# A gated linear recurrence and a maxout feed-forward layer: the same 821 steps in another order, on other engines, in other PSUM banks

## The chip, the cores and the metric

The kernel runs on one core of one Trainium2 chip. Its engines run side by side, each through its own queue in order: TensorE (PE in the profile, with weight loads as PEld), VectorE (DVE), ScalarE (ACT), GpSimd (POOL) and SyncE (SP), which here only issues DMAs. The metric is the device time of one execution in microseconds, as a median over runs. Before the change it is 150.05 us (3 runs: 149.97, 150.05, 151.45).

## The reference

```python
def _attn_ref(q, k, v, alpha):              # each 4 x 8 x 768 x 48
    for t in range(S):
        state = alpha[:, :, t, :, None] * state + np.einsum('bhd,bhe->bhde', k[:, :, t], v[:, :, t])
        y[:, :, t] = np.einsum('bhd,bhde->bhe', q[:, :, t], state)
    return y

def _moe_ref(x, w1, w2, w3, w_out):         # x is 3072 x 384, w1 to w3 384 x 768, w_out 768 x 384
    h = np.maximum(np.maximum(x @ w1, x @ w2), x @ w3)
    return h @ w_out
```

The output y of the first, with its heads side by side, is the x of the second. All arrays are float32.

## The kernel before

**Tiling.** The sequence of 768 is cut into three chunks of 256 rows; with four batches that makes 12 *batches* n (chunk n // 4, batch n % 4), each of two *units* u (four heads each). Inside a batch there are two sub-chunks of 128 rows. The recurrence is computed by blocks of 64 rows: the logarithms of alpha are summed along the rows by a matmul, q and k are scaled by exponentials of the sums, a matmul gives the masked products inside a block, and a carried state per batch gives the part from earlier blocks. The feed-forward layer then takes the 256 rows of a batch. It computes max(x w1, x w2, x w3) as x w1 plus max(0, x(w2 - w1), x(w3 - w1)), and the part x w1 w_out by one product matrix *past*.

**Steps.** The function builds a plan: each call of `plan.step` notes one step (its kind, the engines that may do it, what it reads and writes, its PSUM banks), in 821 numbers. Most steps are one instruction; a PE step is a group of matmuls. For one batch, in order of data flow, with the engine and the line of the instruction:

| kind | what | engine, line |
|---|---|---|
| load | alpha, q, k, v of a batch (halves for batch 0) | SP L278 |
| aa, la | product of neighbouring alphas, logarithms | POOL or DVE L355, ACT L360, L365 |
| hp, e, G | totals, their exponentials, state factors | PE L375, ACT L382, POOL or DVE L387, L392 |
| Lp, L0, exp, exq | sums along rows, and exp(-sum), exp(sum) | PE L430, DVE L434, ACT L445, L448 |
| q, k, v | scaled q, k, v in 16 bits | POOL or DVE L441; v POOL L265 or ACT L263 |
| tp, qkT | transposes of q and k, their copy to SBUF | PE L476, DVE L490 |
| A, LA | products inside a block, masked copy | PE L502, DVE L510 |
| pp, add, Z, Zu | state sums and state update | PE L534, DVE L404, L416, L554, POOL L404, L561 |
| yi, ya | output from the state, and from the block | PE L583, L605 |
| xb, xp, xT | scaled copy, transposing matmul, copy to x | ACT or DVE, PE L626, ACT or DVE L259 |
| gp, h0, h1 | x(w2 - w1) or x(w3 - w1), its maximum | PE L649, ACT L658 or DVE L660, DVE L665 |
| op, ob, out | past and w_out, copy, store | PE L682, L685, ACT or DVE L259, SP L701 |

Once in the kernel there are four weight loads (steps 39, 74, 86, 131; issued by POOL, L292 and L295), six differences of weights (189 to 194, DVE L312), three transposes of w1 (*wt* 195, 197, 199, PE L325, with copies 196, 198, 200) and the product matrix (*mp*, PE L338).

Of the PE steps, tp, A, pp and ya run matmuls with 64 or 48 rows in two halves of the array; hp, Lp, yi, xp, gp, op, wt and mp use all 128 rows.

**The order.** `ORDER` is a string with one token for each step, in the order in which the program is written. A token is the step's number, a letter for its engine (P, V for DVE, A, G for POOL, S) and, for a PE step that opens PSUM banks, a digit for each bank key. `Plan.emit` goes through the tokens and calls each step:

```python
            i, eng, rows = int(token[:at]), ENGINES[token[at]], token[at + 1:]
            ...
            place.update(zip(s["banks"], map(int, rows), strict=True))
            s["run"](eng)
```

So the table alone sets the order inside every engine's queue, the engine of each step that has a choice, and the bank. tp and A take two banks, the one named and the next. The framework adds the waits: an instruction waits for what it reads, and a step that opens a bank waits until what lay in it has been read. A store (out) waits for its output copy on SP, and what stands behind it on SP waits with it; an output copy waits until the store before it has read its buffer (four buffers).

Steps that the prediction names: 1, 2, 4 to 7 are the loads of q, k and v of batch 0, 53 to 56 those of batch 1. 57 is aa and 58, 59 are la of batch 1. 19 and 20 are exp and exq of unit 0, 30 and 31 of unit 1, 65 and 66 of unit 2, 77 and 78 of unit 3; 61 is e of batch 1. 21, 22 are q and k of unit 0; 32, 33, 34 are q, k, v of unit 1. 24, 35, 70 and 82 are tp of units 0 to 3, 27, 38, 73, 85 their LA; 46 and 93 are ya of batches 0 and 1. 124 is tp of units 4 and 5. 226 and 233 are v of batch 4, 241 its pp. 257, 259, 261, 263, 265, 267 are the gp of batch 0, 325 to 335 (odd) those of batch 1. 747 and 763 are gp of batches 8 and 9, 746 and 750 are h1 of batch 8. 791 and 794 are op 20 and 21, 792 and 795 their copies, 793 and 796 their stores; 797 to 807 (odd) are the gp of batch 11, 809 to 818 the last op, 819 and 820 the last copy and store. 543 and 544 are a copy and its store, 614 is the load of v of batch 10 and 637 its reader.

Of the kernel before, what the change touches and what calls it, by code (L numbers as in the profile page):

```python
# [36 lines left out]
209S 162P0 157A 282P2 205P3 163V 283A 164A 158A 201P5 167V 343S 206A 160V 165A 203P3 398A 159V 166G
276S 202V 169P0 228V 204A 136V 161A 220P4 168G 269P5 221V 210S 173V 154G 222A 229A 170V 230A 176P32
171P0 270A 277S 178V 231G 174P6 223A 177V 272P5 175V 224G 278S 172V 337P3 225G 273A 179V 232G 344S
180V 288P7 295P1 181P0 338A 289V 234P4 347G 296V 290A 182P2 238V 411S 297A 340P6 219G 298A 183V 186A  # L40
# [6 lines left out]
431P0 533P5 536A 483G 677S 432V 550A 375P3 534V 427A 463P1 549G 433A 376V 408P5 434A 313G 362A 339S
310V 369G 312V 464V 409A 428G 680S 485A 314V 484A 315V 480S 354G 435G 316P0 317P3 318P 372P4 319A
373V 377P71 476P6 551A 322A 271S 379V 436G 614S 323P4 378V 320P5 552P0 324V 438P2 321A 421G 420G
380V 553A 437A 381G 384P4 442V 486P0 597P7 548S 487A 477A 382V 489G 385P0 439V 422G 386P 491G 383V  # L50
443P5 390A 440P2 478S 488G 387A 537P1 615G 481S 441V 405P0 490G 617A 444V 430G 547S 529P2 423G 598A
538V 599P5 406A 498A 407S 492P3 388P7 679S 618P0 493V 601P1 389A 530V 619A 494A 391P7 555V 621G
# [705 lines left out]
```

## Time and profile before

| what | value |
|---|---|
| median of 3 runs | 150.05 us (149.97 to 151.45) |
| the profiled execution: its time, its span | 151.32 us, 149.6 us |
| VectorE, ScalarE, GpSimd busy | 115.9, 87.4, 73.4 us |
| mean TensorE clock granted, by the profile | 0.997 |
| DMA | 26.34 MB, 176 GB/s over the span |
| last PE matmul ends, span ends | 146.6 us, 149.6 us |

The span runs from the first to the last instruction; 1.7 us lie around it. Times in the profile are from the span's start. "L649 PE MATMUL psum<-xT,d ... x432 | 55.0, 278" is a group of instructions: line, engine, operation, what it writes and reads, count, then busy time in us and mean ns of one. Matmuls are pipelined, so the mean of one is longer than the time that it adds: in the chain of waits, six L649 matmuls behind each other add 0.66 us. In a timeline row the bracket at the end holds the idle time of the engine before the instruction, and what ended it.

### The profile page before, as it was taken

To read this page: it belongs to the slowest core of one execution; us is meant where nothing else is said; L and a number is where in the kernel's file an instruction comes from. 1 tells how busy PE (TensorE), PEld (TensorE's weight loads), DVE (VectorE), ACT (ScalarE), POOL (GpSimd) and SP (SyncE) were. 2 spreads that over 40 slices of the span, in tenths; PEclk is the share of its full clock that TensorE was granted. 3 is DMA by queue.
4 is the path that set the end of the run, shared out by engine and by line. 5 is a ranking of instruction groups with operands and counts; after the bars stand their busy time and mean duration, and the time that the engine had idled before them with its cause. 6 is when DMAs were issued, how large, how long until landed. Compare 5 with 4: busy or idle time off the path is not lost.

```text
span 149.6 us, 5638 instructions
## 1 busy us (share of the span) xinstructions
PE 133.0 (89%) x2389; PEld 103.0 (69%) x2389; DVE 115.9 (77%) x215; ACT 87.4 (58%) x194; POOL 73.4 (49%) x118
## 2 busy tenths in 40 slices
PE   0235798999999999999999999999799999999991
PEld 0014677877766768887888778877579777776861
DVE  6356988499978999999998788979889985656260
ACT  3756236894987498968868787655464123412311
POOL 8159901275235997899982649585456010000000
PEclk9999999999999999999999999999999999999998
DMA  5999999999999999999999992104111010004403
GB/s 121 253 260 264 241 213 224 265 242 214 278 254 260 242 266 256 255 269 266 277 298 273 288 284 57 57 2 161 58 53 57 0 57 0 0 4 158 158 30 127
DMA packets 54728, 26.34 MB, mean 176 GB/s; under 512 B 50736, under 2 KB 54320, under 8 KB 54704
## 3 DMA queue, kind: packets, MB, share of 16 engines
q1 hardware_dynamic: 53584, 23.60, 62.0%
q0 software_dynamic: 832, 2.36, 8.2%
q8 instruction: 18, 0.29, 0.8%
q10 hardware_dynamic: 288, 0.04, 0.2%
q14 instruction: 6, 0.05, 0.1%
HBM read 23.63 MB, written 4.72 MB: 189 GB/s over the span
## 4 chain that ended last, share of the span: by engine, by line
PE 79%; DVE 9%; DMA 5%; SPq 2%; issue 1%; POOL 1%; ACT 1%; DVEq 0%; ACTq 0%; POOLq 0%
PE psum L649 32%; PE psum L685 14%; PE psum L682 7%; PE psum L502 5%; PE psum L476 5%; PE psum L605 4%; DVE LA L510 4%; DMA kn<-in_k_dram 3%; PE psum L626 3%; PE psum L583 2%; SPq L278 2%; PE psum L338 2%; PE psum L534 2%; DVE qkT L490 2%; DMA out_dram<-ob 1%
## 5 line engine op out<-in xcount | busy, mean ns | idle before, releaser
L649 PE MATMUL psum<-xT,d 128*128 128x256 f16 x432 | 55.0, 278 | 0.0
L649 PEld LDWEIGHTS <-d 128*128 128x128 f16 x432 | 41.2, 100 | 6.8
L510 DVE TENSOR_TENSOR LA<-psum,d 128x1024 f16<-128x1024 f32 x24 | 29.0, 1219 | 2.6 <-PE psum L502 1.6
L665 DVE TENSOR_TENSOR hT<-psum,hT 128x512 f16<-128x512 f32 x36 | 23.9, 681 | 6.8 <-PE psum L649 6.5
L685 PE MATMUL psum<-wo,hT 128*128 128x384 f16 (+1 forms) x150 | 27.5, 320 | 0.0
L658 ACT ACTIVATE hT<-psum 128x512 f16<-128x512 f32 x30 | 17.7, 604 | 11.5 <-PE psum L649 10.9
L441 POOL TENSOR_TENSOR qk<-qn,ep 128x384 f16<-128x384 f32 x18 | 18.0, 1004 | 11.7 <-ACT ep L448 8.2
L441 POOL TENSOR_TENSOR qk<-kn,en 128x384 f16<-128x384 f32 x18 | 17.9, 1000 | 7.2 <-DMA kn<-in_k_dram 2.9
L259 ACT COPY ob<-psum 128x384 f32<-128x384 f32 (+1 forms) x18 | 8.3, 463 | 22.0 <-PE psum L685 18.8
L685 PEld LDWEIGHTS <-hT 128*128 128x128 f16 x150 | 14.4, 98 | 9.0 <-DVE hT L665 0.2
L490 DVE COPY qkT<-psum 128x1024 f16<-128x1024 f16 x24 | 15.7, 684 | 3.5 <-PE psum L476 3.1
L682 PE MATMUL psum<-past,xT 128*128 128x384 f16 (+1 forms) x75 | 15.9, 321 | 0.0
L263 ACT ACTIVATE xb<-psum,c 128x384 f16<-128x384 f32 x18 | 9.9, 580 | 8.4 <-PE psum L605 8.3
L259 ACT CAST xT<-psum 128x384 f16<-128x384 f32 x21 | 9.7, 488 | 8.2 <-PE psum L626 8.2
L445 ACT ACTIVATE en<-psum 128x384 f32<-128x384 f32 x24 | 11.5, 490 | 2.8 <-DVE psum L434 2.5
L434 DVE TENSOR_TENSOR psum<-psum,la 128x192 f32<-128x192 f32 x24 | 8.5, 360 | 4.4 <-PE psum L430 3.1
L502 PE MATMUL psum<-qkT 48*64 48x128 f16 x384 | 10.3, 235 | 1.3 <-DVE qkT L490 1.0
L476 PE MATMUL psum<-d,qk 64*128 64x64 f16 x384 | 8.8, 198 | 2.5 <-DVE LA L510 1.4
L561 POOL TENSOR_TENSOR Z<-U,G 48x192 f16<-48x192 f32 x11 | 5.6, 506 | 11.0 <-DVE U L554 10.6
L355 POOL TENSOR_TENSOR aa<-an 128x384 f32<-128x384 f32 x10 | 9.9, 1003 | 1.3 <-DMA an<-in_alpha_dram 1.2
L476 PEld LDWEIGHTS <-qk 64*128 64x128 f16 x384 | 7.4, 99 | 4.0 <-issue 2.8
L375 PE MATMUL psum<-c,la 128*128 128x4 f16 x48 | 3.0, 167 | 8.0 <-ACT la L365 8.0
(61 smaller groups left out, 193.7 us busy)
## 6 DMA issues: line engine op xcount, KB each, us to landing
out_dram<-ob SPq DMA_DIRECT2D x23, 192.0 KB, 2.1
an<-in_alpha_dram SPq DMA_DIRECT2D x11, 384.0 KB, 6.1
vn<-in_v_dram SPq DMA_DIRECT2D x11, 384.0 KB, 6.1
kn<-in_k_dram SPq DMA_DIRECT2D x11, 384.0 KB, 6.3
qn<-in_q_dram SPq DMA_DIRECT2D x11, 384.0 KB, 6.0
wcat<-in_moe_w_dram POOLq DMA_DIRECT2D x2, 576.0 KB, 11.7
w1s<-in_moe_w_dram POOLq DMA_DIRECT2D x1, 576.0 KB, 7.9
wo<-in_moe_w_out_dram POOLq DMA_DIRECT2D x1, 576.0 KB, 8.4
```

Source lines behind the costliest of these rows:

```text
L259: (nc.scalar.copy if eng == "ACT" else nc.vector.tensor_copy)(out=out, in_=in_)
L441: on[eng].tensor_mul(qk[:, w, :, :, :D].rearrange("p r h d -> p h r d"), ld[x][n % NL][:, hs], e)
L445: lambda eng: nc.scalar.activation(out=en, in_=live[Lk], func=AFT.Exp, scale=-1.0),
L476: nc.tensor.transpose(live["tp", v][:, i, at:at + HALF], qks[v % NQ][rows, w, r, 2 * j:2 * j + 2, :], ident[rows, rows])
L490: lambda eng: nc.vector.tensor_copy(out=qkT.rearrange("p i w j t -> p i (w j t)"), in_=live["tp", u]),
L502: nc.tensor.matmul(live[Ak][i * HALF:(i + 1) * HALF, p, at:at + P], qkT[rows, i, 1, j, r * HALF:(r + 1) * HALF], qkT[rows, i, 0, j, :], st ...
L510: lambda eng: nc.vector.tensor_mul(LA.rearrange("p a j r t -> p (a j) (r t)"), live[Ak].rearrange("p a (j t) -> p (a j) t", j=2), maskA.un ...
L649: nc.tensor.matmul(live[gk][:, jj, :], hidden(apart[g][j][:, kt], jj), xT[:, kt, :], start=(kt == 0), stop=(kt == NFT - 1))
L658: nc.scalar.activation(out=h, in_=live[gk], func=AFT.Relu)
L665: lambda eng, h=h, gk=gk: nc.vector.tensor_max(h, live[gk], h),
L682: nc.tensor.matmul(live[ok], xT[:, kt, i * P:(i + 1) * P], past[:, kt, cols], start=(kt == 0), stop=False)
L685: nc.tensor.matmul(live[ok], hT[:, kt, i * P:(i + 1) * P], wo16[:, kt, cols], start=False, stop=(kt == NJ - 1))
```

## The change

Only the string `ORDER` changes. All steps are the same. Every engine has the steps in another order. 79 steps are on another engine: among them 9 of the v from ACT to POOL and 6 the other way; 8 output copies from ACT to DVE and 3 back; 7 of the h0 from ACT to DVE and 5 back; 5 of the q each way between DVE and POOL, 2 of the k each way; aa of batch 1 from DVE to POOL. DVE gets 206 steps (200 before), ACT 184 (193), POOL 106 (103). PE keeps its 248, in another order and in other banks, and SP its 77. Among the loads, those of q, k and v of batches 0 and 1 and alpha of batches 3 and 4 change places; the stores stand elsewhere among the loads.

```diff
@@ -24,49 +24,49 @@
...
 ORDER = """
-0S 3S 1S 53S 7S 2S 5S 6S 8V 10A 4S 11V 12A 13A 56S 14P0 28P4 17P1 15A 9A 29V 16G 18V 30A 55S 19A 57V
-31A 20A 59A 21V 54S 60P5 22G 63P6 75P2 61A 58A 24P0 32G 64V 100S 25V 65A 33G 76V 26P3 77A 101S 34G
-27V 62G 23G 69A 39G 35P4 81A 102S 78A 40P37 74G 36V 66A 86G 42V 37P4 41V 80G 103S 38V 45P1 46P0 68G
-79V 67G 44V 87P45 47A 43V 50A 88V 90V 70P1 82P6 71V 51P0 83V 72P1 52A 84P6 73V 145S 104G 195P3 89V
-48P2 106A 91V 199P4 105A 85V 92P1 49A 117P5 200A 118V 93P6 189V 107P7 108A 97V 119A 257P4 109G 94A
-191V 110P1 120A 95P6 111V 98P7 190V 265P2 96A 99A 207S 197P6 112A 325P7 266A 193V 113A 121G 333P2
-198A 275S 114V 261P5 192V 258A 329P6 115V 326A 122V 147S 196A 124P0 194V 334A 263P4 128V 116G 262A
-146S 125V 131G 129P2 330A 267P7 130V 123A 149G 150A 132P06 148S 133V 126P2 134V 331P1 212A 127V 211G
-259P5 151A 137P0 213A 332V 138P2 264V 327P3 208S 142A 260V 139A 143P0 279G 155P1 144A 268V 140P4
...
-226G 235V 291A 345S 285G 349A 299G 292V 236P3 348A 184P5 187P1 237V 399P2 341A 287G 185A 545S 401P7
-188A 233G 400V 356P0 241P46 293G 402A 357V 239P1 242V 412S 358A 465P3 243V 244G 240V 466A 245G 403P4
...
-542P7 456P6 543V 603P5 457A 510V 568A 544S 684P4 631P6 725P7 604V 563G 726A 632V 569G 508P2 509V
-513P5 511P0 685A 682A 661P7 633A 729P4 662V 636G 733P2 514V 730A 515V 727P7 734A 516V 517G 512V
...
-643P6 590A 645P5 644V 640P1 699A 608P4 700A 702G 641V 695G 747P6 609A 587V 751P1 610S 748A 647V
-591P0 588P4 752A 649G 749P6 592V 689G 696A 589V 743P1 646V 750V 735P7 648G 686V 701G 761P5 736V
-745P0 744V 762A 763P6 703A 746V 753P4 704P1 754V 740P0 708V 705V 764V 769P7 741A 742S 711P1 706P5
-712V 709P3 707V 755P0 714G 713V 765P5 710V 756A 716P6 758P0 766A 715V 770V 651P5 717P7 759V 650P1
-652P 718P 656A 771P0 653A 657P5 767P1 772V 658A 654P3 737P0 655A 722V 768V 783P5 738V 779P1 784A
-787P0 780V 781P5 788V 776P1 719V 785P0 777A 789P7 778S 786V 739S 723P6 760S 773P4 790V 782V 720P1
-794P3 774V 721A 724A 803P6 795V 799P5 796S 775S 805P7 757S 801P3 806A 807P1 802A 797P0 808V 791P3
-798V 800V 804V 809P1 792V 810P 793S 813P3 811A 814P 812S 817P2 815A 816S 818P 819A 820S
+0S 3S 53S 5S 1S 2S 7S 4S 8V 6S 12A 11V 10A 54S 9A 17P4 13A 18V 14P2 28P0 57G 15A 29V 55S 59A 19A
+63P2 75P3 58A 60P5 56S 22V 61A 20A 64V 76V 21G 77A 100S 30A 34G 24P4 31A 62G 65A 33G 25V 23A 102S
+66A 26P4 32G 78A 27V 101S 39G 35P0 16G 79V 40P57 68G 36V 103S 41V 67G 37P0 42V 44V 45P6 74G 38V 70P3
+81G 104G 71V 207S 80V 72P1 86G 106A 82P3 73V 69G 46P0 83V 87P25 50A 47A 84P3 88V 105A 89V 51P6 117P1
+85V 195P2 52A 48P6 196A 197P0 91V 118V 49A 92P2 43V 119A 93P6 198A 189V 199P7 190V 94A 107P4 110P0
+191V 97A 95P6 108A 90V 98P3 111V 265P4 109G 200V 112A 145S 96V 99A 257P7 113A 194V 266A 261P5 193V
+120A 147S 267P6 122V 115V 329P2 114G 121V 331P4 146S 330A 268V 131G 124P0 332V 116A 333P6 125V 123G
+148S 128V 126P3 334A 211G 127V 258A 129P1 325P6 262A 208S 212A 130V 132P30 149G 213A 335P5 326A 133V
+214P4 263P7 151A 134V 215A 150A 136V 152P1 162P2 216G 137P3 192V 138P4 264V 259P6 142A 135V 153A
...
+272P6 338V 290A 296V 291A 277S 179V 297A 180V 292G 182P5 298A 273V 234P3 186A 284G 479S 285G 340P1
+183A 299G 235V 226A 238V 233A 219G 345S 184P3 187P2 341V 347G 185A 241P54 239P6 188A 243V 236P0 415G
+240V 465P2 349A 545S 401P3 466A 245G 242V 403P6 348A 237V 287G 344S 402A 397P2 244G 417A 404V 293G
...
+368G 481S 353G 360G 469P3 471P5 470A 472V 252P6 253A 255P2 416A 304P3 305V 256A 309P10 311V 310V
+274S 313G 413S 312G 367G 307P6 308V 461P5 462A 535P2 536A 395P4 531P1 316P5 315V 463P7 532A 414S
...
+442V 390A 498G 495A 388P1 497G 406V 678S 389A 496G 615G 677S 503G 391P7 392A 440P3 441V 443P5 445P12
+659P7 447V 663P0 660A 444V 601P3 571A 505A 597P4 664A 602V 407S 564G 552P5 599P6 475S 598A 446V 680S
...
+633A 456P2 621G 624P3 604V 665P4 556G 457A 636G 576V 542P2 625V 573V 626A 634A 666V 729P5 543A 635G
+544S 508P6 730A 513P4 614S 509V 511P0 627A 733P5 683A 628G 725P2 512V 734A 629G 690P3 682A 731P6
+726A 515V 697P1 727P0 514V 698V 674P2 516G 691V 699A 728V 554G 692A 517G 732V 693A 519P0 700A 518P7
+675V 637A 520P 701G 676S 638P5 521A 524V 574P1 642V 695G 639V 694G 577P3 579P0 735P7 578V 522P6
...
+743P3 610S 646V 686V 620V 740P7 705V 744A 648G 708V 746V 591P0 751P1 647V 588P3 753P2 752V 649G 589A
+689G 592A 747P4 754V 703A 749P6 748V 765P3 741V 750V 761P1 742S 673S 766V 767P4 650P5 763P6 768V
+762V 769P7 771P2 764V 770A 716P0 772V 706P3 711P1 709P6 707V 758P2 712V 710V 755P3 759V 714V 760S
+773P7 713V 756A 715V 757S 607S 717P4 651P2 718P 652P 719V 776P1 656A 653V 657P2 654P3 777A 737P5
+658V 655A 778S 722A 783P6 738V 785P1 739S 784V 723P2 720P0 786V 779P3 789P5 780A 774V 787P6 721A
+775S 724A 781P7 788A 805P0 782V 799P6 790V 806A 797P1 807P5 798V 803P2 800V 791P1 808V 801P6 794P4
+802A 804V 809P6 795A 792A 793S 810P 796S 813P1 811A 814P 812S 817P0 815A 816S 818P 819A 820S
```

More of the change, by code (lines that the diff above doesn't have):

```diff
@@ L37 @@
[L37 to L40, printed above, removed]
-226G 235V 291A 345S 285G 349A 299G 292V 236P3 348A 184P5 187P1 237V 399P2 341A 287G 185A 545S 401P7
@@ L47 @@
[L47 to L52, printed above, removed]
@@ new lines @@
+120A 147S 267P6 122V 115V 329P2 114G 121V 331P4 146S 330A 268V 131G 124P0 332V 116A 333P6 125V 123G
+148S 128V 126P3 334A 211G 127V 258A 129P1 325P6 262A 208S 212A 130V 132P30 149G 213A 335P5 326A 133V
+214P4 263P7 151A 134V 215A 150A 136V 152P1 162P2 216G 137P3 192V 138P4 264V 259P6 142A 135V 153A
+139A 143P3 336V 155P1 154G 327P0 275S 144A 163V 156V 227P3 140P5 328V 220P7 157A 203P4 164A 260V
+209S 165A 167V 201P0 158A 160V 204A 159G 141A 228V 205P6 276S 166V 202A 221V 161A 168G 169P1 206V
+229A 210S 217G 176P54 173V 218G 230A 269P0 222A 178V 231G 177V 223A 343S 170V 224G 174P5 270A 171P1
@@ new lines @@
+393P7 172V 279G 411S 337P3 394A 175V 281A 232G 280A 278S 288P1 282P7 181P2 225G 289V 295P0 283A
+272P6 338V 290A 296V 291A 277S 179V 297A 180V 292G 182P5 298A 273V 234P3 186A 284G 479S 285G 340P1
+183A 299G 235V 226A 238V 233A 219G 345S 184P3 187P2 341V 347G 185A 241P54 239P6 188A 243V 236P0 415G
+240V 465P2 349A 545S 401P3 466A 245G 242V 403P6 348A 237V 287G 344S 402A 397P2 244G 417A 404V 293G
+363P7 350P0 356P3 398A 399P1 342S 357V 351A 364V 482S 358A 418P2 300G 467P5 247V 365A 246V 359A
+248P6 400V 249P0 294G 419A 250P 346S 468V 301G 302P1 251A 286G 366A 306V 254A 421G 412S 361G 303V
@@ new lines @@
+368G 481S 353G 360G 469P3 471P5 470A 472V 252P6 253A 255P2 416A 304P3 305V 256A 309P10 311V 310V
+274S 313G 413S 312G 367G 307P6 308V 461P5 462A 535P2 536A 395P4 531P1 316P5 315V 463P7 532A 414S
+314V 396V 422G 317P3 424P2 318P 369A 362G 425V 370P0 464V 322A 548S 355G 533P6 426A 374V 549G 427A
+323P3 371V 527P7 324A 534V 483G 319A 377P43 339S 372P0 551A 271S 379V 375P5 550A 428G 611S 373V
+408P2 485A 528A 352G 354G 480S 376V 484A 476P0 409V 613S 378V 431P2 537P1 380V 477A 430G 382V 499P7
+432V 320P0 420G 486P5 538V 529P6 381G 321A 433A 423G 500V 473P0 547S 383V 434A 429G 530V 435V 436G
@@ new lines @@
+492P3 501A 384P1 410S 385P4 474V 487A 546S 386P 493V 504G 438P5 387A 405P0 502A 439V 612S 437G 494A
+442V 390A 498G 495A 388P1 497G 406V 678S 389A 496G 615G 677S 503G 391P7 392A 440P3 441V 443P5 445P12
+659P7 447V 663P0 660A 444V 601P3 571A 505A 597P4 664A 602V 407S 564G 552P5 599P6 475S 598A 446V 680S
+449G 553A 558P7 593P0 451V 555G 448G 667P3 559V 679S 600V 489G 560A 565P1 661P5 490V 561A 563G 566V
+668A 669P6 594V 478S 616A 662V 539P3 567A 562V 568A 617A 670V 595P0 450V 681G 569V 631P7 453P2 452P6
```

15 lines of the change are left out of this document (3 added, 12 removed).

## The prediction

> **What bounds the kernel now.** I read the page's busy shares first, then the chain that ended last, then the stretches, then the start instruction by instruction.
>
> ```profile
> PE 133.0 (89%) x2389; PEld 103.0 (69%) x2389; DVE 115.9 (77%) x215; ACT 87.4 (58%) x194; POOL 73.4 (49%) x118
> PE 79%; DVE 9%; DMA 5%; SPq 2%; issue 1%; POOL 1%; ACT 1%; DVEq 0%; ACTq 0%; POOLq 0%
> ```
>
> TensorE (PE) is busy for 133.0 of 149.6 us and holds 79% of the chain. The stretches show where its idle time lies (the columns are PE, PEld, DVE, ACT and POOL busy time, then clock and DMA):
>
> ```profile
> 30.00:60.00 30.00, 29.65 (x617) 22.11 (x615) 27.42 (x50) 23.26 (x55) 19.18 (x28) 1.00 1.09 252
> 60.00:90.00 30.00, 29.96 (x585) 24.16 (x584) 26.65 (x51) 23.86 (x55) 22.17 (x36) 1.00 1.08 276
> 90.00:123.00 33.00, 32.11 (x614) 24.99 (x605) 28.87 (x49) 16.77 (x36) 16.86 (x25) 1.00 0.16 54
> 89.04:125.13 36.09, 35.20 (x667) 27.32 (x665) 31.63 (x52) 18.27 (x40) 17.28 (x25) 1.00 0.18 58
> ```
>
> From 30 to 123 us PE is idle for only 0.35 + 0.04 + 0.89 = 1.28 us. Its 16.6 us of idle time (149.6 - 133.0) are thus nearly all in the first 30 us and behind its last matmul. After 30 us a table can gain two things: those 1.28 us, and PE time that depends on which step follows which.
>
> ```profile
> 24.92 1.41 PE psum L649 x6
> 27.13 1.28 PE psum L649 x6
> 29.05 2.81 PE psum L649 x24
> 60.29 0.66 PE psum L649 x6
> 104.96 0.35 DVE U L554
> 105.38 0.52 POOL Z L561
> 144.72 1.89 DMA out_dram<-ob
> 146.69 0.32 ACT ob L259
> ```
>
> These rows of the chain (start, duration, what) give three facts. Six L649 matmuls take 1.41 and 1.28 us before 28.4 and 0.66 later (24 of them 2.81 us from 29.05): TensorE runs at half pace up to about 29 us, though the clock column shows 1.00 there. The one long stall after 37 us is the state chain U, Z at 104.96. And the end is a tie: the last output copy waits for a store that lands at 146.61, where PE is just done.
>
> **The order on TensorE.** Steps tp, A, pp and ya use half of the array's rows, the others all of them.
>
> ```profile
> 56.34 0.23 PE psum L502 x16
> 67.91 0.35 PE psum L502 x16
> 68.25 0.76 PE psum L649 x6
> ```
>
> An A step behind another half-array step (pp, 56.34) adds 0.23 us; behind a full-array step (67.91) 0.35; and the gp step behind it 0.76 instead of 0.66. Going into a run of half-array steps and out of it thus costs 0.12 + 0.10 = 0.22 us. Counted from step 124 (tp of unit 4, the 37th PE step in both tables, with as many gp steps ahead of it) to the end, the old table has 25 such runs and the new one 20. Five fewer: 5 x 0.22 = **1.1 us less**. Three more runs vanish ahead of step 124; PE waits for data there, so I count nothing.
>
> **The start.** Rows of the timeline; the bracket is the idle time before and what ended it.
>
> ```profile
> 3.86 0.36 DVE L355 TENSOR_TENSOR aa<-an 128x192 f32<-128x192 f32 x1 [0.43 <-DMA an<-in_alpha_dram]
> 4.58 0.36 DVE L355 TENSOR_TENSOR aa<-an 128x192 f32<-128x192 f32 x1 [0.35 <-DMA an<-in_alpha_dram]
> 6.30 0.87 ACT L445 ACTIVATE en<-psum 128x384 f32<-128x384 f32 x2
> 7.06 0.50 ACT L448 ACTIVATE ep<-psum 128x384 f32<-128x384 f32 x1
> 7.58 0.56 DVE L355 TENSOR_TENSOR aa<-an 128x384 f32<-128x384 f32 x1 [1.02 <-DMA an<-in_alpha_dram]
> 8.06 0.55 DVE L441 TENSOR_TENSOR qk<-qn,psum 128x384 f16<-128x384 f32 x1
> 8.17 0.52 ACT L365 ACTIVATE la<-aa 128x384 f16<-128x384 f32 x1 [0.24 <-DVE aa L355]
> 9.14 1.00 POOL L441 TENSOR_TENSOR qk<-kn,en 128x384 f16<-128x384 f32 x1 [2.94 <-DMA kn<-in_k_dram]
> 10.19 0.40 PE L476 MATMUL psum<-d,qk 64*128 64x64 f16 x8 [0.51 <-POOL qk L441]
> 10.63 0.69 DVE L490 COPY qkT<-psum 128x1024 f16<-128x1024 f16 x1 [0.49 <-PE psum L476]
> 11.37 0.64 PE L502 MATMUL psum<-qkT 48*64 48x128 f16 x16 [0.79 <-DVE qkT L490]
> 12.14 1.23 DVE L510 TENSOR_TENSOR LA<-psum,d 128x1024 f16<-128x1024 f32 x1 [0.55 <-POOL qk L441]
> 13.42 0.61 PE L476 MATMUL psum<-d,qk 64*128 64x64 f16 x16 [1.40 <-DVE LA L510]
> 18.42 1.04 PE L476 MATMUL psum<-d,qk 64*128 64x64 f16 x32 [0.57 <-ACT xb L263]
> 23.90 0.82 PE L605 MATMUL psum<-v,LA 64*128 64x48 f16 x32 [0.38 <-DVE LA L510]
> 27.75 0.56 DVE L312 TENSOR_TENSOR d<-wcat,w1s 128x768 f16<-128x768 f16 x1 [0.40 <-DMA wcat<-in_moe_w_dram]
> 31.79 0.64 PE L476 MATMUL psum<-d,qk 64*128 64x64 f16 x32
> L355 POOL TENSOR_TENSOR aa<-an 128x384 f32<-128x384 f32 x10 | 9.9, 1003 | 1.3 <-DMA an<-in_alpha_dram 1.2
> ```
>
> The loads of batch 0 and 1 change places on SP. Half loads land 0.72 apart (3.86, 4.58), so step 53 (alpha 1), now ahead of q, lands at about 6.85 instead of 7.56. Its product (57) goes from DVE (0.56) to POOL (1.00): done at 7.85, not 8.14. But ACT now has la (59) ahead of the first exp (19), and ACT is in order: 59 runs 7.87 to 8.40, and exp ends at 8.9 where both first ones were done by 7.17; 58 (as long as 59), a small 61 and exp 20 (0.50) follow, to 10.0. The q product of unit 0 (21) moves to POOL (1.00) and waits for 20: 10.05 to 11.05. Then tp (24, 0.61) to 11.7, where it ended at 10.59; copy 0.69, A 0.64, LA 1.23: LA (27) ends at 14.4 instead of 13.37. The next tp (35) waited 1.40 us for that LA because of its bank; in another bank, it now waits for POOL, which has three products and a v in a row (21, 34, 33, 32: 13.8), and starts at 13.85, against 13.42. From there the new table recovers: tp of unit 2 goes ahead of the ya of unit 0 and starts at 16.8 (now 18.42). LA of unit 3 (85) ends near 23.0, so ya (93) starts behind the transposes wt 195 and 197, at 24.3 (now 23.90, where LA held it for 0.38). All three wt stand ahead of the first gp, which starts at 27.2. Of six gp steps, 1.6 then run at 1.28 us until 29.3 and 4.4 at 0.66: step 124 starts at 27.2 + 2.1 + 2.9 = 32.2 instead of 31.79: **+0.4 us**. The weights' issues on POOL move back by 0.5 to 4 us (w1 behind two products more); their transfers queue one behind the other in any case, so I count nothing. That cover is thin: now the third weight lands at 27.7, and its first reader (194) is reached at 28.8, for step 267 at 29.9. From 2 us of delay on, PE waits.
>
> **Stalls after the start.** The 1.28 us go. New ones, by following DVE, ACT and POOL in their new order with the durations above: A of unit 5 waits for the second of two copies, 0.4 (the old table paid that for unit 4); pp of batch 4 (241) waits for v on ACT, where 226 and 233 come from POOL to stand behind two xb, 0.4; three waits of 0.1 to 0.15 at steps 304, 535 and 445, 0.4; gp 747 and 763 take the banks that h1 746 and 750 empty late, behind two copies on DVE, 0.5. Sum 1.7: **+0.4 us** net. Bounds: 0, if each is hidden, and the next part's price.
>
> **DVE.**
>
> ```profile
> L259 DVE COPY ob<-psum 128x384 f32<-128x384 f32 x7 | 3.9, 555 | 1.9 <-PE psum L685 1.1 <-DMA out_dram<-ob 0.4 <-ACT v L263 0.3
> L660 DVE TENSOR_SCALAR hT<-psum 128x512 f16<-128x512 f32 x6 | 4.1, 687 | 1.7 <-PE psum L649 1.6
> ```
>
> DVE gets 206 planned steps instead of 200: five more output copies (5 x 0.555) and two more h0 (2 x 0.687), 4.1 us, the other swaps cancel to about nothing. ACT and POOL have room. Of the 4.1 us, 1.6 fall in the start and 2.2 on the PE steps 150 to 215, the stretch 89.04 to 125.13, in which DVE is busy 31.63 of 36.09: 33.8 of some 35. I take it as hidden but for the 0.5 above.
>
> **Stores and the end.** The store of step 793 waits for the output copy 792, which moves from DVE (last there) to ACT, behind copy 795. PE's last op steps no longer have gp 797 and op 791 just ahead; counted back from PE's end, 792 is done 1.97 us earlier, and 1.89 more for the store is again a tie with PE's end. **0**, with 0.1 either way. The other stores move among loads on SP; DMA's 5% of the chain is the first loads and the last store, so no load in between was on the path. The cover to watch is load 614 (v of batch 10): it is queued on SP behind the store of copy 543, so it goes out near 96 us, and its reader 637 comes some 4 us after its landing: 0.
>
> **Sum.** -1.1 + 0.4 + 0.4 + 0 = -0.3 us. The profiled execution took 151.32 us (span 149.6, 1.7 around it), so it would take 151.0. It stands 1.27 over the median 150.05; the runs spread by as much (149.97 to 151.45). Taken to the median: 149.8.
>
> **The clock, weighed with the skill.** PE was busy 3.04 of the 3.42 us before 25.89 and the pace stayed slow; it changed after 3.41 busy us to 29.30.
>
> ```profile
> 22.47:25.89 3.42, 3.04 (x52) 1.00 1.03 216
> 25.89:29.30 3.41, 3.41 (x25) 1.00 1.07 261
> ```
>
> The Trainium skill (TensorE: Matmul & The Clock Gate, Part 1) says that the clock is released by a busy window of about 3.4 us that runs freely, so its place differs from run to run; the trace agrees as far as one execution can. The same page (Part 4: PE-mode transpose) says that transposes don't count as busy; by that, three wt in a row at 22 to 25.7 would not bring the release forward, and the sum stays 149.8; without that rule it would be 148.7. No run here shows which.
>
> **Rivals.** *Faster:* the change of pace comes one stretch of 3.4 us earlier, at 25.9, since PE has fewer gaps and the three wt ahead of it. The six gp are then bound by DVE's d and q products, and step 124 starts at 31.1: -1.1; with the bank waits of 0.5 hidden as well, 148.2. For it: PE's gaps from 18.4 on are 0.1 to 0.2 us, against 0.38 now. Against it: gp starts 2.3 us later than today's first (24.92). *Later clock:* the gaps before gp push the change of pace back by a stretch: 3.4 us at half pace, +1.7: 151.5. *Slower:* DVE becomes the bound on PE steps 150 to 215. If DVE needs the 4.46 us of idle time that it has there today (waits for PE's own results), its 2.2 us more lengthen the stretch by 2.2: 152.0. It decides once DVE's idle time cannot fall under 2.3 us. For it: 747 and 763 have no slack. Against it: in 30 to 60 DVE is busy 27.42 of 30 and PE lost 0.35. *The merged runs give nothing:* 150.9, inside the forecast's range.
>
> **Numbers.** Forecast 0.42 (149.8; its own range 148.6 to 151.3), faster rival 0.27, later clock 0.10, DVE 0.21. About 1% (1.5 us) is what a measurement of this kernel can tell from no change. Faster by more: 0.27. Slower: 0.21 and half of the later clock, 0.26. Within: 0.47. The range 147.9 to 152.3 takes in both rivals' times.
>
> **What would show it.** Right: step 124's tp (first L476 x32) at 32.2; L649 x6 at 0.66 from 29 to 30 us; 20 runs of half-array steps after it; PE idle 1 to 2 us from 32 to 123; no store in the last wait. Wrong: a first tp before 11 us (the ACT order costs nothing), PE idle over 3 us between 89 and 125 with DVE as its releaser, or a pace that changes in another stretch.

## The result, and the profile after

The new table takes 147.95 us (147.51 to 148.50 in 4 runs), the old one 150.24 beside it: ratio 0.9851, 95% interval 0.9814 to 0.9888, so 1.5% faster. The forecast of 149.8 ("within 1%") did not come; the time is that of its faster rival (148.2). The profiled execution took 147.51 us, span 145.8, against 151.32 and 149.6. That pair differs by 3.8 us and the medians by 2.1 (from the 150.05 measured first) to 2.3 (from 150.24), since before's profiled execution was 1.1 to 1.3 over its median and this one 0.44 under. What follows divides the 3.8. Ratios, here and below, compare only executions within 1.5% of the fastest of their kernel, while a median is that of all its executions, so that the two need not agree.

From the page after: busy shares, and the chain that ended last.

```profile
PE 129.4 (89%) x2389; PEld 102.1 (70%) x2389; DVE 116.6 (80%) x221; ACT 82.3 (56%) x185; POOL 75.5 (52%) x121
PE 71%; DMA 16%; SPq 9%; POOL 1%; issue 1%; ACT 0%; ACTq 0%; POOLq 0%
```

The stretches after (columns as before):

```profile
30.00:60.00 30.00, 29.60 (x620) 22.20 (x619) 27.57 (x52) 24.32 (x57) 22.14 (x33) 1.00 1.11 253
60.00:90.00 30.00, 30.00 (x646) 24.74 (x645) 28.28 (x53) 20.83 (x47) 24.85 (x38) 1.00 1.07 278
90.00:123.00 33.00, 33.00 (x561) 25.90 (x560) 30.40 (x53) 14.57 (x33) 13.13 (x20) 1.00 0.15 46
19.10:22.52 3.42, 3.24 (x103) 2.79 (x98) 3.23 (x5) 1.86 (x4) 0.41 (x1) 1.00 1.07 229
22.52:25.93 3.41, 3.41 (x61) 3.11 (x59) 2.76 (x7) 3.09 (x7) 0.00 (x0) 1.00 1.05 213
```

PE is idle for 0.40 us between 30 and 123, all of it before 60; 1.28 before. DVE is no bound: from 60 to 123 PE lost nothing. The pace changed at 25.93, behind a stretch without a gap; in the old kernel at 29.30.

Three steps divide the difference: tp 124, tp 169 (units 6 and 7) and the last op step (818). The rows of the new kernel, then of the old one (its 124 is in the prediction):

```profile
30.59 0.64 PE L476 MATMUL psum<-d,qk 64*128 64x64 f16 x32
42.01 0.64 PE L476 MATMUL psum<-d,qk 64*128 64x64 f16 x32
142.15 0.66 PE L685 MATMUL psum<-wo,hT 128*128 128x192 f16 x6
142.89 0.32 ACT L259 COPY ob<-psum 128x192 f32<-128x192 f32 x1 [0.42 <-PE psum L685]
```

```profile
44.44 0.74 PE L476 MATMUL psum<-d,qk 64*128 64x64 f16 x32
145.94 0.66 PE L685 MATMUL psum<-wo,hT 128*128 128x192 f16 x6
```

| stretch | old | new | difference |
|---|---|---|---|
| to tp 124 | 31.79 | 30.59 | -1.20 |
| tp 124 to tp 169 | 12.65 | 11.42 | -1.23; gp 393, gp 397 and hp 282 now stand behind 169 and Lp 220 ahead, 1.33 us of work: +0.10 for the same work |
| tp 169 to the last three matmuls (818: 146.27, 142.48) | 101.83 | 100.47 | -1.36; with that work, -2.69 |

The -2.69 is, by the median time of each kind of step before a half-array or a full-array neighbour: -0.85 for 16 runs of half-array steps instead of 21 (0.17 each), -1.05 for the wait at yi 584, and -0.79 for delays of 0.06 to 0.11 us at single steps (1.58 in all in the old kernel, 0.79 in the new), mostly in and beside such runs. The split between the first and the third depends on the sorting: with the neighbours on both sides of a step counted, they come out as -1.29 and -0.35.

### The profile page after: what moved, and what is told of

Its sections match the earlier page's. It is cut to its first block, busy times and chain, and to the rows that moved or that the text cites. A ratio compares the mean times of both kernels' runs of the same rounds, so it can differ in the third digit from the quotient of the medians.

```text
span 145.8 us, 5641 instructions
## 1 busy us (share of the span) xinstructions
PE 129.4 (89%) x2389; PEld 102.1 (70%) x2389; DVE 116.6 (80%) x221; ACT 82.3 (56%) x185; POOL 75.5 (52%) x121
## 4 chain that ended last, share of the span: by engine, by line
PE 71%; DMA 16%; SPq 9%; POOL 1%; issue 1%; ACT 0%; ACTq 0%; POOLq 0%
PE psum L649 28%; PE psum L685 16%; DMA qn<-in_q_dram 10%; PE psum L682 9%; SPq L278 9%; DMA wo<-in_moe_w_out_dram 6%; PE psum L502 4%; PE psum L605 3%; PE psum L476 3%; PE psum L626 2%; PE psum L338 2%; PE psum L583 2%; PE psum L534 2%; POOL qk L441 1%; PE psum L430 1%
## 5 line engine op out<-in xcount | busy, mean ns | idle before, releaser
L649 PE MATMUL psum<-xT,d 128*128 128x256 f16 x432 | 53.1, 273 | 0.0
L649 PEld LDWEIGHTS <-d 128*128 128x128 f16 x432 | 40.4, 98 | 5.9 <-issue 0.2
L658 ACT ACTIVATE hT<-psum 128x512 f16<-128x512 f32 x28 | 16.4, 597 | 18.7 <-PE psum L649 17.7
L441 POOL TENSOR_TENSOR qk<-qn,ep 128x384 f16<-128x384 f32 x18 | 18.6, 1035 | 11.0 <-ACT ep L448 8.1
L441 POOL TENSOR_TENSOR qk<-kn,en 128x384 f16<-128x384 f32 x18 | 18.0, 1013 | 0.6 <-ACT en L445 0.5
L263 ACT ACTIVATE xb<-psum,c 128x384 f16<-128x384 f32 x19 | 10.8, 585 | 7.6 <-PE psum L605 7.6
L355 POOL TENSOR_TENSOR aa<-an 128x384 f32<-128x384 f32 x11 | 11.0, 1007 | 4.3 <-DMA an<-in_alpha_dram 4.1
L259 ACT COPY ob<-psum 128x384 f32<-128x384 f32 (+1 forms) x13 | 5.8, 454 | 12.9 <-PE psum L685 8.8
L430 PE MATMUL psum<-la,c 128*128 128x192 f16 x24 | 6.2, 267 | 7.4 <-ACT la L365 7.4
L365 ACT ACTIVATE la<-aa 128x384 f16<-128x384 f32 (+1 forms) x13 | 6.5, 498 | 6.7 <-POOL aa L355 6.7
L502 PEld LDWEIGHTS <-qkT 48*64 48x64 f16 x384 | 6.9, 114 | 4.7 <-DVE qkT L490 3.7
```

The lines of the kernel that those rows point to most:

```text
L259: (nc.scalar.copy if eng == "ACT" else nc.vector.tensor_copy)(out=out, in_=in_)
L441: on[eng].tensor_mul(qk[:, w, :, :, :D].rearrange("p r h d -> p h r d"), ld[x][n % NL][:, hs], e)
L502: nc.tensor.matmul(live[Ak][i * HALF:(i + 1) * HALF, p, at:at + P], qkT[rows, i, 1, j, r * HALF:(r + 1) * HALF], qkT[rows, i, 0, j, :], st ...
L649: nc.tensor.matmul(live[gk][:, jj, :], hidden(apart[g][j][:, kt], jj), xT[:, kt, :], start=(kt == 0), stop=(kt == NFT - 1))
L658: nc.scalar.activation(out=h, in_=live[gk], func=AFT.Relu)
```

## The experiments

A step's *lag* is its start in a run less its start in the kernel it was made from. Ratios are to the old kernel.

**Half the table each.** *s_start* has the new table's tokens up to 124, then the old one's; *s_rest* the reverse. Banks that would clash:

```diff
-325P7 333P2 263P4
+325P3 333P6 263P7
...
-267P6
+267P7
```

> The new table up to step 124 (its first 36 PE steps), the old order, engines and banks behind it (banks of 325, 333 and 263 chosen anew). Theory 1: the new start is worth 1.2 us, because TensorE's pace changes one stretch of 3.4 us earlier; then the pace changes near 25.9, tp 124 starts near 30.6, and the time is 150.05 - 1.2 = 148.85 (ratio 0.992). Theory 2: the start gains nothing of its own in the unprofiled runs, and the whole 2.1 us come from the order behind 124; then 150.0 (1.000).

> The old table up to step 124, the new one behind it (bank of 267 chosen anew). Theory 1: the pace changes near 29.3, tp 124 starts near 31.8, and only what lies behind 124 is gained: 2.1 - 1.2 = 0.9 us by the medians, up to 2.6 by the two profiled runs, so 147.5 to 149.15, 149.1 the likeliest (ratio 0.994). Theory 2: the whole gain is here: 148.0 (0.986). From 124 to the last op step the trace should show about 112 us, as in the new kernel (111.9), not 114.5, by either theory.

Measured: s_start 153.14 (1.0184, 1.0139 to 1.0228), s_rest 150.98 (1.0039, 1.0003 to 1.0074). Neither theory's time came, and neither half brings its share: each swap adds waits of its own at the seam, so the two times do not tell which half holds the gain. In s_start tp 124 starts at 32.31, since the old table has gp 325 and 333 ahead of it, on top of the new table's six, and PE waits 0.47 us there. In s_rest the new table wants gp 267 early, whose d step 194 the old start makes late; PE waits 0.72, 0.88 and 0.73 us in two stretches. Its pace was then taken back:

```profile
28.71:32.12 3.41, 2.68 (x25) 2.10 (x23) 2.42 (x6) 3.41 (x8) 1.29 (x2) 1.00 1.19 253
32.12:35.54 3.42, 1.63 (x70) 1.10 (x69) 3.42 (x6) 2.13 (x5) 1.96 (x2) 1.00 1.15 243
35.54:38.95 3.41, 3.41 (x53) 2.62 (x53) 2.04 (x4) 0.69 (x2) 0.20 (x1) 0.50 1.25 277
```

After a stretch with 1.63 of 3.42 us busy, the clock column has 0.50 for the next one, 1.7 us of work lost. What the two runs do show is how the rest behaves (start of a step, us):

| step | new kernel | s_rest | c_new_wt | c_fill |
|---|---|---|---|---|
| A 174 | 44.52 | 47.98 | 44.98 | 44.54 |
| op 340 | 50.30 | 53.75 | 50.76 | 50.31 |
| A 508 | 93.49 | 96.94 | 93.94 | 96.14 |
| op 818 | 142.48 | 145.92 | 142.93 | 145.13 |

From 45 us on, s_rest keeps its lag of 3.45 us to 0.02 over 95 us: the rest runs like clockwork, and what differs from run to run comes before (but for c_fill and b_prod, below). A price behind 45 us can so be read from one execution by the lag.

**The pace and the transposes.** *c_old_wt* and *c_new_wt* move wt 197:

```diff
-118V 93P6 ... 95P6 ... 207S 197P6
+118V 197P6 93P0 ... 95P0 ... 207S
...
-196A 197P0 91V ... 93P6 198A 189V ... 331P4 146S 330A
+196A 91V ... 93P6 189V ... 331P4 197P3 146S 330A 198A
```

> The old table with one PE step moved: the transposes wt 197 go ahead of ya 93, where PE stood idle for 0.38 us (banks of 93 and 95 chosen anew). Theory 1, a stretch of 3.41 us without a gap changes the pace, transposes count as work: the stretch 22.5 to 25.9 is then filled, the pace changes at 25.9, tp 124 starts at 30.6 to 30.9, 148.9 (ratio 0.992). Theory 2, transposes do not count, or the gap is not what held the pace: it changes at 29.3 or one stretch later, 150.0 to 151.5 (1.000 to 1.010).

> The new table with the same step moved the other way: wt 197 goes from ahead of yi and ya of batch 1 to behind gp 331, about where the old table has it (bank 3). ya 93 can then start at 23.4, and its xb and xp leave PE idle for 0.2 to 0.4 us before 25.9. Theory 1: the pace then changes at 29.3, and 3.4 us run at half pace more: 147.95 + 1.2 to 1.7 = 149.2 to 149.6 (ratio 0.994 to 0.997). If the gap closes after all, 25.9 and 147.95. Theory 2, the pace did not hang on this step: 147.95 (0.986), whatever gap the trace shows.

Measured: c_old_wt 151.40 (1.0013, 0.9979 to 1.0047), c_new_wt 148.49 (0.9885, 0.9852 to 0.9919). Theory 1 fails in both: the pace changed at 28.02 in the one, at 26.74 in the other (there behind 3.06 of 3.41 us busy), and neither time followed. In c_old_wt the stretch from 24.60 to 28.02 was wholly busy; but the stretches do not lie where the theory had put them. Where it changes moves from execution to execution. In five profiles with the old start (the old kernel, c_old_wt, s_rest and, below, b_fix and b_prod) it is 29.30, 28.02, 25.30, 28.43, 26.75, mean 27.6; in five with the new one (the new kernel, c_new_wt, r_split, a_dve, n_best) 25.93, 26.74, 23.87, 22.89, 24.78, mean 24.8. So the new start brings it forward by 2.7 us on average, though the two sets overlap (s_start's trace has no record of it). In the profiled execution of c_old_wt something else took the time, DVE's rows first, then POOL's, then PE's:

```profile
30.74 1.32 DVE L441 TENSOR_TENSOR qk<-kn,en 128x384 f16<-128x384 f32 x2
31.98 2.87 DVE L312 TENSOR_TENSOR d<-wcat,w1s 128x768 f16<-128x768 f16 x1
34.78 1.27 DVE L490 COPY qkT<-psum 128x1024 f16<-128x1024 f16 x2
30.61 1.05 POOL L265 TENSOR_SCALAR v<-vn,c 128x384 f16<-128x384 f32 x1 [1.61 <-DMA vn<-in_v_dram]
31.61 0.82 POOL L292 DMA_DIRECT2D wo<-in_moe_w_out_dram  x1
32.47 1.97 POOL L355 TENSOR_TENSOR aa<-an 128x384 f32<-128x384 f32 x2
35.51 0.64 PE L502 MATMUL psum<-qkT 48*64 48x128 f16 x16 [2.34 <-DVE qkT L490]
```

A 0.55-us subtraction (194) takes 2.87: it ends at 34.85, 0.42 behind the second of POOL's two aa, and PE waits 2.34 for the copy behind it. PE then lost the pace for two stretches. That execution took 155.47 us, 4.1 over its kernel's median: this explains the long execution, not the median.

**The price of a run of half-array steps.** *r_split*, eleven moves like these:

```diff
-393P7 (behind 171P1)      -461P5 (behind 307P6)
+393P7 (ahead of 171P1)    +461P5 (ahead of 307P6)
```

> The new table with eleven of its merged runs of half-array steps taken apart again: a full-array step that stood beside the run is put between two of its members (393 ahead of 171, 340 of 234, 461 of 307, 533 of 370, 527 of 372, 405 of 438, 733 of 513, 735 of 577, 608 of 643, 758 of 711, 776 of 652). 20 runs become 31, the work is the same. Theory 1, each run costs 0.22 us on TensorE: the lag of each step behind its time in the new kernel grows by 0.22 at each of eleven places between 44 and 125 us, 2.4 us in all, and the time is 150.4 (ratio 1.002). Theory 2, the neighbours on TensorE do not matter: the lag stays where it stands at 44 us, 147.95 (0.986).

Measured: 155.59 (1.0321, 1.0258 to 1.0384), far over both. At the five places where nothing waits behind the split, the lag grows by 0.11, 0.19, 0.20, 0.20 and 0.16, mean 0.17. One of them, new kernel first:

```profile
60.95 0.42 PE L534 MATMUL psum<-v,qk 64*64 64x48 f16 x32
61.20 0.43 PE L502 MATMUL psum<-qkT 48*64 48x128 f16 x16
61.55 1.70 PE L649 MATMUL psum<-xT,d 128*128 128x256 f16 x14
```

```profile
63.82 0.42 PE L534 MATMUL psum<-v,qk 64*64 64x48 f16 x32
64.17 0.83 PE L649 MATMUL psum<-xT,d 128*128 128x256 f16 x6
64.93 0.42 PE L502 MATMUL psum<-qkT 48*64 48x128 f16 x16
65.28 1.49 PE L649 MATMUL psum<-xT,d 128*128 128x256 f16 x12
```

pp, A and the way back take 0.60 us together; apart 0.35 + 0.35, and the gp between 0.76 instead of 0.66. The lag grows by 7.6 us behind 45 us; more than half of it is idle time that the new kernel doesn't have. PE's waits from 45 us on (engine, tile, line, what for: us in total, times, longest):

```profile
PE psum L626 <- DVE qkT L490: 1.4, 1, 1.4
PE psum L626 <- ACT xb L263: 0.7, 1, 0.7
PE psum L502 <- DVE qkT L490: 0.6, 2, 0.4
PE psum L682 <- DVE LA L510: 0.5, 1, 0.5
```

They stand behind half-array steps that come one gp later, and whose copy, LA or xb then comes later too. So theory 1 holds with 0.17 for 0.22, and keeping half-array steps together is worth more where it also starts a chain earlier.

**The long wait, and d step 194.** *b_fix* is the old table with

```diff
-193V 113A 121G ... 124P0 194V 334A
+193V 194V 113A 121G ... 124P0 334A
...
-697P3 584P0 580V 525P4 671P5
+697P3 580V 525P4 671P5 584P0
```

> The old table with two moves. (a) d step 194 on DVE goes from behind 115 to right behind 193, out of the way of POOL's v 116, the issue of w_out (131) and two aa, beside which it took 0.86 us in the old kernel and 2.87 in the run with wt 197 moved, where PE then waited 2.34 us and lost the pace for 6.8 us. (b) yi 584 goes behind op 671 on PE, so that the state chain U, Z has 1.6 us more. Theory 1: the long runs of the old kernel (up to 156.2) come from (a), so that the runs stay below 151.5, and (b) takes 0.9 to 1.05 us off between 105 and 110 us; 149.1 (ratio 0.99). Theory 2: the spread comes from elsewhere and stays, and the wait at 584 only moves to yi 585 or ya 586: 150.0 (1.00).

Measured: 150.31 (0.9962, 0.9923 to 1.0001); lag -0.12 up to 104 us and -0.96 from 107 to the end: (b) is 0.84 of the 1.05 above, about the idle time of the first row here; in the second kernel op 671 fills it.

```profile
105.92 0.34 PE L583 MATMUL psum<-Z,qkT 128*128 128x96 f16 x4 [0.89 <-POOL Z L561]
```

```profile
105.14 0.65 PE L682 MATMUL psum<-past,xT 128*128 128x384 f16 x3
105.62 1.14 PE L685 MATMUL psum<-wo,hT 128*128 128x384 f16 x6
106.60 0.50 PE L583 MATMUL psum<-Z,qkT 128*128 128x96 f16 x8
```

Of 74 runs of the old kernel over all sessions 17 took more than 152.1 us; of the 22 runs of b_fix and b_prod, which have 194 moved, none did. That fits (a), but it is argued, not shown: no execution among those 17 was profiled.

**DVE's slack, and w_out earlier.** *a_dve* is the new table with

```diff
-114G 121V 331P4 146S 330A 268V 131G
+131G 114G 121V 331P4 146S 330A 268V
...
-543A 609A 672A 756A
+543V 609V 672V 756V
```

> The new table with two edits that are read apart by the lag of each PE step behind the new kernel: up to 45 us the first, from 90 us on the second. (a) The issue of w_out (131, POOL) goes ahead of q product 114: mp 203 no longer waits 0.31 us for the load. Rival: its transfer takes part of the 16 DMA engines from the q load of batch 2, which then lands up to 1 us later, and tp 124 with it. (b) Four more output copies (543, 609, 672, 756) go from ACT to DVE, 4 x 0.555 = 2.2 us more there between 92 and 124 us. If DVE were the bound in that stretch, as one rival of the prediction had it, PE's lag grows by up to 2.2 us there; if DVE has slack, by less than 0.2. Time 147.6 to 148.0 (0.984 to 0.986) with slack and without the rival, 150.2 (1.001) with DVE as the bound.

Measured: 151.88 (1.0042, 0.9995 to 1.0089). (a) The rival, and worse: alpha and k of batch 3 land later (36.86 and 38.32, for 33.56 and 34.80 in the new kernel), PE waits 1.67 us for la, loses the pace for one stretch, and lags 4.58 at 49 us. (b) Between 109 and 130 us the lag grows by 0.77 for 2.2 us of DVE work: DVE had about 1.4 us left there. It is not the bound, but near it.

```profile
38.91 0.25 PE L375 MATMUL psum<-c,la 128*128 128x4 f16 x4 [1.67 <-ACT la L365]
92.00:124.00 32.00, 31.64 (x618) 25.73 (x620) 30.18 (x55) 13.81 (x31) 13.64 (x22) 1.00 0.19 58
```

**An earlier pace by fillers.** *c_fill*, in the steps A (units 2, 3) and pp (batch 1):

```diff
+            for _ in range({2: 12, 3: 1}.get(u, 0)):
+                nc.tensor.matmul(live[Ak][:, 0, :P], ident, ident, start=True, stop=True)
...
+            if n == 1:
+                nc.tensor.matmul(live[keys[0]].rearrange("p a b -> p (a b)")[:, :P], ident, ident,
+                                 start=True, stop=True)
```

> The new kernel with 14 added matmuls of constants (128x128, 0.107 us each at half pace) that fill PE's gaps from 16.4 to 22 us: 12 ahead of A of unit 2, where PE waits 1.30 us, one ahead of pp of batch 1 and one ahead of A of unit 3. They write into banks that the step behind them overwrites; the output is the same. Theory 1, a stretch of 3.41 us without a gap changes the pace: it changes one or two stretches earlier, at 19.1 or 22.5 instead of 25.9. What it is worth depends on what else sets the first gp step: by the run with the new start and the old rest, where the pace changed near 23.3 and gp 257 began only 0.25 us earlier, 0.2 to 0.4 us, 147.6 (ratio 0.983). Theory 2, TensorE alone sets the start: half of the 3.4 to 6.8 us that are no longer slow, 1.7 us or more, 146.2 (0.974). If added matmuls of constants do not count, 25.9 and 147.95.

Measured: 149.57 (0.9899, 0.9858 to 0.9940). The pace changed at 21.16, 4.8 us earlier, and the lag at A 174 is 0.02: theory 2 falls, an earlier pace alone is worth nothing to the new table. The first gp starts at 26.84, for 26.38 in the new kernel, behind waits of 0.17 to 0.26 us for ACT's copies, and tp 124 at 30.86 behind six gp. The 2.65 us come between 52 and 90 us, where loads land late: the v load issued at 47.86 (47.30 in the new kernel) lands at 55.59 (53.21). The DMA engines moved less in this execution (new kernel first):

```profile
52.00:56.00 4.00, 4.00 (x99) 3.44 (x97) 3.74 (x6) 3.33 (x8) 3.85 (x6) 1.00 1.11 263
```

```profile
52.00:56.00 4.00, 3.96 (x95) 3.15 (x93) 3.73 (x6) 3.30 (x8) 3.42 (x5) 1.00 0.82 206
```

Whether the fillers had part in that is open; nothing between them and these loads shows a link.

**Pace against products in the old start.** All three from b_fix. *b_prod* makes the products of batch 2 earlier; *b_pace* adds fillers by step (*b_both* has both):

```diff
-112A 325P7 266A 193V 194V 113A
+112A 325P7 113A 266A 193V 194V
...
-192V 258A 329P6 115V 326A 122V
+258A 329P6 115V 326A 122V 192V
```

```diff
+FILL = {35: 13, 37: 2, 45: 1, 70: 5, 48: 1, 93: 3}
...
+            for _ in range(FILL.get(i, 0)):
+                self.fill(place[s["banks"][0]])
             s["run"](eng)
```

> The old table with the two moves of the run before (194 behind 193, 584 behind 671; call it the mended old table: pace changed at 28.4, product 122 ended at 31.97, tp 124 began at 31.54), and 25 added matmuls of constants that fill PE's gaps from 12 to 24 us (13 ahead of tp 35, 2 of A 37, 1 of yi 45, 5 of tp 70, 1 of xp 48, 3 of ya 93; each writes into the bank that its step overwrites). Theory 1, the late pace is what the old start loses: the pace changes between 17 and 25, tp 124 starts at 30.6 or earlier, and PE's lag behind the mended table is -0.9 or more from 45 us on. Theory 2, the products of batch 2 (114, 115, 122 on DVE, last at 31.4 to 32.0) hold tp 124 in any case: PE gets idle ahead of 124 instead, and the lag is 0 to -0.3.

> The mended old table with the products of batch 2 made earlier, and no fillers: on ACT, exq 113 goes ahead of relu 266; on DVE, d step 192 goes behind product 122. 122 should end at 30.5 to 30.9 instead of 31.97. Theory 1 (pace): PE is busy at half pace up to 28.4 and has work up to 31.5 in any case, so tp 124 stays at 31.4 to 31.6 and the lag at 0, plus or minus 0.2. Theory 2 (products): tp 124 at 30.6 to 31.0, lag -0.6 to -0.9 from 45 us on.

> The mended old table with both: the fillers and the earlier products. If only one of the two holds tp 124, this run equals the better one of the two single runs. If both do, one behind the other, the single runs gain 0 to -0.3 each and this one gains what the new start has, tp 124 at 30.6 and a lag of -0.9 to -1.3 from 45 us on; 149.1 to 149.4 by the median of 150.3 of the mended table.

Measured: b_pace 154.79 (1.0275, 1.0227 to 1.0323), b_both 153.99 (1.0204, 1.0133 to 1.0274), b_prod 150.45 (0.9996, 0.9961 to 1.0031). The first and the last design failed: tp 35 waits for LA because of its bank, and fillers into the same bank wait with it and then run ahead of it, so the start came 2.3 to 2.7 us later. They tell nothing on the pace. In b_pace:

```profile
13.38 1.55 PE L733 MATMUL psum<-d 128*128 128x128 f16 x13 [1.40 <-DVE LA L514]
```

In b_prod the last product (122) ended at 30.82 instead of 31.97, the pace changed at 26.75, tp 124 started at 31.31 and the lag was -0.37 (later +0.66, after a wait at 81 us). Beside the other runs:

| kernel | pace changes | last product of batch 2 ends | tp 124 starts |
|---|---|---|---|
| old | 29.30 | 31.42 | 31.79 |
| b_fix | 28.43 | 31.97 | 31.54 (second unit waits) |
| b_prod | 26.75 | 30.82 | 31.31 |
| new | 25.93 | 30.53 | 30.59 |
| c_new_wt | 26.74 | 30.91 | 30.91 |
| n_best | 24.78 | 30.72 | 30.27 (second unit waits) |
| c_fill | 21.16 | 30.41 | 30.86 |

In the old table 2.55 us of earlier pace, with products that end 0.60 earlier, bring tp 124 forward by 0.48: much of it turns into idle time (from 24 to 45 us PE idles 0.33, 0.68, 1.09 us in the first three rows). In the new kernel and c_new_wt tp 124 follows the products within 0.06 us; in c_fill it follows the six gp.

**A version meant to beat both.** *n_best*, the new table with relus 258 and 262 and gp 335 earlier:

```diff
-330A 268V 131G 124P0 332V 116A 333P6 125V 123G 148S 128V 126P3 ... 213A 335P5
+258A 262A 330A 268V 131G 124P0 332V 116A 333P6 125V 123G 148S 128V 335P5 126P3 ... 213A
```

> The new table with PE's waits of 0.15 and 0.35 us at A 126 and A 129 (32.1 and 32.7 us) covered: on ACT, relu 258 and 262, whose gp steps are done at 28.0 and 28.7, go ahead of relu 330 into an idle time of 1.16 us, which empties the bank of 335, and gp 335 goes ahead of A 126. From 45 us on, the lag of the new kernel was constant to 0.02 us in a run that differed before 35 us only, so what PE gains there should be kept to the end: lag -0.5, 147.45 (ratio 0.982). Rival: LA of A 126 and 129 come 0.05 to 0.45 later and ya 138, the next to need them, waits instead: lag 0 to -0.2. A load that lands late between 45 and 90 us, as in the run with fillers (there 2.6 us), would hide either.

Measured: 148.50 (0.9873, 0.9824 to 0.9922), not told apart from the new kernel; lag +0.40 from 45 us on. The gain did not come, and not by the rival either: this time DVE's product 115 ran into POOL's 114. DVE's row, then POOL's, then PE's:

```profile
28.43 1.82 DVE L441 TENSOR_TENSOR qk<-kn,en 128x384 f16<-128x384 f32 x2
28.74 1.10 POOL L441 TENSOR_TENSOR qk<-qn,ep 128x384 f16<-128x384 f32 x1 [2.23 <-ACT hT L658]
30.77 0.62 PE L476 MATMUL psum<-d,qk 64*128 64x64 f16 x31 [0.30 <-DVE qk L441]
```

The two products take 1.82 instead of 1.02 us, and the next one (121) ends at 30.72 instead of 30.14. In the new kernel's execution the q load landed 0.4 us later (28.98 for 28.61), and it was POOL that waited for DVE: 114 took 1.42 us.

## Why the prediction was right or wrong

**In short.** The measured 147.95 lies only just inside the range of 147.9 to 152.3, and it does so because that range was drawn to take in the times of the rivals, the faster one too. The sum itself, -0.3 us, stands against -2.1 to -2.3 by the medians and -3.8 in the profiled pair: of its three terms that are not zero, the start and the stalls have the wrong sign, and only the order on TensorE went as reasoned. The sign of being wrong "a pace that changes in another stretch" came. That the rival's 25.9 met 25.93 is partly luck: with the new start the change fell anywhere from 22.89 to 26.74.

**The start (+0.4; measured -1.20): wrong, at the step "until 29.3".** The chain up to the first gp was right to within 0.8 us and always a little too late: tp 24 ended at 11.36 (forecast 11.7), LA 27 at 14.20 (14.4), tp 35 started at 13.38 (13.85), tp of unit 2 at 16.36 (16.8), ya 93 at 24.18 (24.3), the first gp at 26.38 (27.2). Then the pace had changed at 25.93, as in the faster rival. On PE: busy at half pace for 12.92 us instead of 16.94, 4.02 less, which is worth -2.0; idle time before 24 us 13.01 for 12.36, +0.65, and none in either from there to tp 124; the sum -1.36 is a little more than was measured. The rival was right that products bind next: those of batch 2 end at 30.53, 0.9 earlier than in the old kernel (POOL has one of them, and on ACT their exq stands ahead of the relus). But it took DVE's for the last. The last is POOL's 114, which waits for its q load:

```profile
29.11 1.42 POOL L441 TENSOR_TENSOR qk<-qn,ep 128x384 f16<-128x384 f32 x1 [2.47 <-DMA qn<-in_q_dram]
```

In all seven profiles with the new start (the new kernel, s_start, c_new_wt, r_split, a_dve, c_fill, n_best) this load lands between 28.61 and 29.08 and the product starts 0.13 to 0.14 us behind it, whatever the pace. So in the new order a load, which no term and no rival of the prediction had on the path, limits what an earlier pace can bring; its issue now stands behind that of k (a swap that the list of changed loads does not name), and it lands 1.0 us later than in the old kernel (27.96). How the 1.2 us divide between pace and products was not shown: the runs that should have told failed. The forecast compared one execution's place of the change with another's; it moves by up to 4 us between executions with the same start.

**The order on TensorE (-1.1; measured -0.85): right in mechanism, the price 0.17 instead of 0.22.** 20 runs against 25 from tp 124 on (ahead of it one vanishes, 3 for 4, not three); r_split shows 0.11 to 0.20 for each. Not foreseen: small delays at single steps, most of them in and beside such runs, fell by 0.8 us with them; no run took these apart.

**Stalls after the start (+0.4; measured about -1.7): wrong in size and sign.** The old waits went, the 1.05 at yi 584 among them. Of the new ones (A of unit 5 0.4, pp 241, steps 304, 535 and 445, gp 747 and 763) only A of unit 5 came (0.35, with 0.15 at unit 4); from 60 us on there is none. Following each engine's queue with the old durations piled up small delays that buffers absorb. One came that was not foreseen: mp 203 waits 0.31 us for w_out, whose issue stands behind product 114 on POOL. These rows of the chain are start, duration, what:

```profile
13.88 15.09 DMA qn<-in_q_dram
29.11 1.37 POOL qk L441
30.48 8.47 DMA wo<-in_moe_w_out_dram
38.99 1.14 PE psum L338 x6
```

**DVE (hidden but for 0.5): right** that it is no bound, and hidden wholly; but the 4.1 us more did not come: the copies and h0 do add 4.1, while the other swaps, taken as nothing, take most of it back, and DVE is busy for 116.6 us instead of 115.9. The slack left in a_dve (1.4 us) shows how near the slower rival was. **Stores and the end (0): right**, no store in the last wait. **The rival "merged runs give nothing"** is refuted by r_split, the **later clock** did not come.

**The clock and transposes.** 2.04 of the 3.41 us before the change were busy with transposes (wt), and 0.48 of the stretch before that, which did not change the pace:

```profile
19.10:22.52 3.42, 0.48 (x5) 1.00 1.07 229
22.52:25.93 3.41, 2.04 (x16) 1.00 1.05 213
```

Without wt and tp, PE's rows cover 2.14 us of the stretch that changed the pace and 2.74 of the one that did not. If transposes did not count, the emptier stretch would have changed it. So the trace speaks against the Trainium skill (TensorE: Matmul & The Clock Gate, Part 4: PE-mode transpose) and for the sum without that rule. It does not settle it: much of the other stretch is half-array steps, and no run shows how these count.

## What to carry to other kernels

Read a table's gain behind the start by the lag of single steps: where TensorE has no idle time left, lags stay constant to hundredths of a us, and each saved wait or switch is kept to the end. Keep steps that use half the array together, and start the chains that wait for another engine (A, copy, LA) in the same stroke. Do not judge halves of an order by swapping them: here the seam cost more than either half was worth. And do not count an earlier full pace as time won before you have seen what TensorE would wait for next.

## What the runs showed of the hardware

- **DVE behind POOL.** In the traces of this case a DVE operation with both inputs in SBUF (L312, and L441 with k and en) takes 0.55 us alone, and up to 1.41 beside POOL's work, in two cases even 2.41 (b_both) and 2.87 (c_old_wt). Of 21 that were stretched to 0.85 us or more, 20 ended 0.40 to 0.43 us behind the end of a POOL operation; LA (1.20 to 1.23 us in every trace) and the copies, with their input in PSUM, never stretched. The Trainium skill (SBUF — State Buffer, Summary: rules for kernel authors) says so of two SBUF inputs beside a GpSimd operation that reads SBUF: the second to issue blocks until the first has finished. The traces agree with the blocking. They do not agree in the order: the operation of 2.87 us started at 31.98, while POOL issued a DMA and ahead of both of its aa (32.47 and later), and ended behind them.
- **The pace can be lost mid-kernel** without a long idle time: after 1.63 of 3.41 us busy (s_rest, c_old_wt), with no single gap over 0.9 us in the first, and after 1.75 (a_dve); the emptiest stretch that kept it had 2.09 (r_split, 51.17 to 54.59). What share is enough to get it stays open: 3.05 of 3.42 us was (s_rest, at 25.30); 3.04 and 3.32 of 3.41 (old kernel, up to 25.89 and 22.47) and 3.24 (new kernel) were not.
- **Loads** keep the DMA engines busy up to 85 us (a share of 0.8 to 1.2 in stretches of 4 us from 40 to 72), and what they move differs between executions: 206 GB/s from 52 to 56 us in c_fill against 263 in the new kernel, and c_fill fell 2.65 us behind between 52 and 90.
